# A spectral mixer with a GEGLU FFN on one core: LN1 reordered per quad, matmuls on zeros, W loaded in two halves, the last inverse n1 transform behind the first FFN chunk

## The chip, the cores and the metric

The kernel runs on one core of one Trainium2 chip. The time is device microseconds (us) of that core, lower is better.

The engines are TensorE (PE in the profile, with PEld for its weight loads), VectorE (DVE), ScalarE (ACT), GpSimd (POOL) and SyncE (SP). SyncE only issues transfers here; GpSimd issues the FFN's weight loads. The profile counts one set of 16 DMA engines for all transfers, whoever issues them. The granted clock is the share of full speed that TensorE's throttle lets through. LN1 and LN2 are the two layernorms, an eviction is a copy of matmul results out of PSUM, where TensorE leaves them, and a warm TensorE is one at full clock, a cold one at half.

## The reference, cut to what matters

```python
h  = x + irfft2(rfft2(layernorm(x)) * (w_r + 1j * w_i))          # x: 2048 x 576
h2 = h + (gelu(ln_h @ w_gate) * (ln_h @ w_up)) @ w_down           # ln_h = layernorm(h); 576 -> 4608 -> 576
```

The Fourier transforms are done as matmuls with tables. The kernel goes through these parts: LN1 and a transform along n1 (16 tiles in four quads), a transform along d and the product with W (16 groups), the inverse transforms (16 tiles), and the FFN in four blocks of 512 rows, each with 36 gate/up chunks of 18 matmuls and then the down matmuls.

## The kernel before

The first part works quad by quad: statistics on VectorE (three tiles) and ScalarE (one tile), a square root on ScalarE, a reciprocal, the scaling of the table ATS on GpSimd, 20 matmuls into PSUM, and five evictions into U.

```python
    ln1_act(0); ln1_stats(0); ln1_sqrt(0)
    ln1_act(1); ln1_stats(1); ln1_scale(0); ln1_sqrt(1)
    a_quad(0, (ACT, ACT, ACT, ACT, ACT))         # 20 matmuls, 5 evictions
    ln1_act(2); ln1_stats(2); ln1_scale(1); ln1_sqrt(2)
    a_quad(1, (ACT, ACT, DVE, ACT, DVE))
    # ... cut: quads 2 and 3 in the same way
```

SyncE issues x, the tables FT, BT and VT, then W in 18 loads, then the tables DT and IT. GpSimd waits for IT and DT and then issues the FFN's weights: gate and up (WGU), and the down weights (WD) once the place of U and W is free.

```python
    for pl, src in ((0, A_w_r), (1, A_w_i)):
        for jj in range(4):
            # ... cut: two loads per jj, 16 partitions x 16 (or 15) groups x 289 elements
            P.dma(SP, WS[jj:64:4, :, pl, 0:K2], a, f"w{pl}", r=["Wz"], w=[("W", pl, jj)])
    # ... cut
    P.op(POOL, None, r=["IT", "DT"])              # GpSimd waits
    for j in range(9):
        P.dma(POOL, WGU[0:64, :, f0:f1], wgv[:, :, f0:f1], f"wg{j}", w=[("WG", j, 0)])
        P.dma(POOL, WGU[64:128, :, f0:f1], wuv[:, :, f0:f1], f"wg{j}", w=[("WG", j, 1)])
    P.alias(ukeys + wkeys + [...], [("WD", j) for j in range(9)])
    for j in range(9):
        P.dma(POOL, WD[:, 4 * j:4 * j + 4, :], wdv[:, 4 * j:4 * j + 4, :], f"wd{j}", w=[("WD", j)])
```

During the inverse transforms the first four tiles are normalized and transposed on TensorE into HT0. Gate and up matmuls use 64 rows of TensorE each, so both partition halves need all of HT. A pair of transfers per tile copies what the other half has.

```python
    def turn_pe(c):
        # ... cut: five transposes on TensorE into PSUM, one eviction on VectorE
        P.dma(SP, HT0[0:64, 5:9, t0:t1], HT0[64:128, 0:4, t0:t1], f"tr{c}", r=[("HT", 0, c, 0)], w=[("HT", 0, c, 1)])
        P.dma(SP, HT0[64:128, 5:9, t0:t1], HT0[0:64, 1:5, t0:t1], f"tr{c}", r=[("HT", 0, c, 0)], w=[("HT", 0, c, 2)])

    for c in range(NT + 1):
        if c < NT:  st_I(c)                       # inverse along d
        if c >= 1:  st_N(c - 1)                   # inverse along n1, residual, sums for LN2
        # ... cut: LN2 of quads 0 to 2, norm() and turn_pe() of tiles 0 to 3
    ln2_a(3); ln2_b(3); ln2_c(3)
```

## Time and profile before

| | before |
|---|---|
| time, median of 4 runs | 532.30 us (531.28 to 533.65) |
| span of the profiled run | 530.8 us |
| first 128-wide matmul of the front | 12.42 us |
| first 289-wide matmul (transform along d) | 33.15 us |
| first 288-wide matmul (inverse along d) | 79.17 us |
| first gate/up matmul | 106.41 us |
| first down matmul | 176.5 us |

These are the rows of the profile page in 40 slices of 13.3 us: TensorE's busy tenths, its granted clock in tenths, the share of the DMA engines and what they moved.

```profile
PE   0379989999999999999999999999999999999997
PEclk9999999999999999999999999999999999999999
DMA  8979999401110000011100000111000000000000
GB/s 325 217 181 216 219 219 319 135 6 26 26 26 12 7 19 18 13 25 27 26 9 7 18 18 14 24 26 27 11 12 17 18 1 1 1 2 1 12 18 17
```

From slice 8 on (106 us) TensorE is full until the end, and the DMA engines are nearly idle; in the first seven slices the DMA engines are busy for 70% or more. All that can be won lies ahead of 106 us. The next lines are TensorE's timeline in the front (start, length, instruction, and in brackets how long the engine had been idle and for whom).

```profile
12.42 2.45 PE L426 MATMUL PS<-ATS,XO 128*128 128x128 bf16 x20 [12.42 <-POOL ATS L418]
...
33.15 4.99 PE L475 MATMUL PS<-FT,U 128*128 128x289 bf16 x20 [0.73 <-ACT U L438]
...
42.15 1.41 PE L475 MATMUL PS<-FT,U 128*128 128x289 bf16 x10
```

Twenty 289-wide matmuls take 4.99 us at first and ten take 1.41 us later, so the early ones run at little more than half the rate. The clock row shows 9 all along: the records of this run begin only at 38.9 us, so it says nothing of the time before.

The chain that ended last, from the fourth tile's eviction on (start, length, what):

```profile
102.65 0.74 DVE HT_69 L610
...
103.41 0.59 SPq L193
...
104.04 2.13 DMA HT_69<-HT_69
...
106.41 70.11 PE PS L649 x648
```

The FFN starts when the last copy of HT has landed, 2.13 us after it was issued. The two issue lines of W are (x9 each; shortest, median and longest issue in ns; first and last start):

```profile
L193 SPq DMA_DIRECT2D WS<-in_A_w_r_dram x9: 608/699/2300, 4.9 to 12.7; - x9
L193 SPq DMA_DIRECT2D WS<-in_A_w_i_dram x9: 595/609/684, 13.7 to 19.0; - x9
```

The table IT was issued at 20.3 us and landed 8.6 us later, near 28.9 us, GpSimd issued its first weight load soon after, and the first packet of WGU moved at 31.5 us:

```profile
29.85 0.92 POOL L193 DMA_DIRECT2D WGU<-in_B_w_gate_dram  x1
```

The last packet of WD moved at 97.8 us. In a window amid that stream the DMA view shows (packets, MB and share by queue; below it a transfer with its us from issue to landing):

```profile
q0 software_dynamic: 286, 1.17, 102.5%
...
HT_69<-HT_69 SPq DMA_DIRECT2D x2, 64.0 KB, 5.5
```

Queue q0 is GpSimd's, q1 SyncE's. The copies issued at 92.42 us and 93.14 us moved nothing in this window; they landed after 5.5 us (median of the two).

### The profile page before, as it was taken

How to read it: one execution, taken by the hardware profiler on the slowest of the kernel's cores; microseconds unless marked ns; L12 is line 12 of the kernel's file. 1: busy time of each engine (PE TensorE's matmuls, PEld its weight loads, DVE VectorE, ACT ScalarE, POOL GpSimd, SP SyncE). 2: the span in 40 equal slices, each digit the busy share in tenths (PEclk: the TensorE clock that was granted, in tenths of full speed). 3: DMA queues.
4: the chain of work that ended last, by engine and by line, in shares of the span. 5: the costliest groups of instructions: out<-in, count | busy, mean ns of one | idle time of the engine just before them, and what ended most of it. 6: DMA issues, size and time to landing. Idle time of an engine off the chain costs nothing.

```text
span 530.8 us, 10113 instructions
## 1 busy us (share of the span) xinstructions
PE 500.6 (94%) x4388; PEld 301.1 (57%) x4388; DVE 185.9 (35%) x427; ACT 151.1 (28%) x280; POOL 26.8 (5%) x40
## 2 busy tenths in 40 slices
PE   0379989999999999999999999999999999999997
PEld 0356757655555777444447774444477744444776
DVE  5337775844333211343332113433311133333111
ACT  4535557843323100233330003223300033332000
POOL 2182013000000000000000000000000000000000
PEclk9999999999999999999999999999999999999999
DMA  8979999401110000011100000111000000000000
GB/s 325 217 181 216 219 219 319 135 6 26 26 26 12 7 19 18 13 25 27 26 9 7 18 18 14 24 26 27 11 12 17 18 1 1 1 2 1 12 18 17
DMA packets 34395, 30.75 MB, mean 58 GB/s; under 512 B 21008, under 2 KB 29328, under 8 KB 34352
## 3 DMA queue, kind: packets, MB, share of 16 engines
q0 software_dynamic: 4176, 15.93, 12.5%
q1 hardware_dynamic: 30032, 13.66, 10.2%
q8 instruction: 34, 0.56, 0.4%
q10 hardware_dynamic: 144, 0.52, 0.3%
q14 instruction: 9, 0.07, 0.0%
HBM read 23.67 MB, written 2.36 MB: 49 GB/s over the span
## 4 chain that ended last, share of the span: by engine, by line
PE 91%; DVE 4%; DMA 1%; ACT 1%; POOL 1%; issue 0%; SPq 0%; DVEq 0%; POOLq 0%
PE PS L649 53%; PE PS L662 27%; PE PS L475 4%; PE PS L552 3%; PE PS L426 1%; PE PS L489 1%; DVE ST_53 L399 1%; PE PS L508 1%; DMA XO<-in_A_x_dram 1%; POOL ATS L418 1%; ACT U L438 1%; PE PS L512 1%; DVE XO L564 1%; PE PS L561 0%; DMA HT_69<-HT_69 0%
## 5 line engine op out<-in xcount | busy, mean ns | idle before, releaser
L653 ACT ACTIVATE GL<-PS 128x512 bf16<-128x512 f32 x144 | 86.0, 597 | 298.1 <-PE PS L649 295.4
L654 DVE TENSOR_TENSOR AT<-GL,PS 128x512 bf16<-128x512 bf16 x144 | 98.8, 688 | 169.5 <-ACT GL L653 169.5
L662 PE MATMUL PS<-WD,AT 128*128 128x288 bf16 x1152 | 141.8, 286 | 0.0
L649 PE MATMUL PS<-HT_69,WGU 64*128 64x512 bf16 x1296 | 140.2, 376 | 0.4 <-DMA HT_69<-HT_69 0.4
L649 PE MATMUL PS<-HT_83,WGU 64*128 64x512 bf16 x1296 | 140.2, 376 | 0.0
L662 PEld LDWEIGHTS PS<-WD,AT 128*128 128x128 bf16 x1152 | 112.4, 98 | 29.9 <-issue 1.7
L649 PEld LDWEIGHTS PS<-HT_69,WGU 64*128 64x128 bf16 x1296 | 68.3, 94 | 71.9 <-issue 0.9
L649 PEld LDWEIGHTS PS<-HT_83,WGU 64*128 64x128 bf16 x1296 | 62.9, 94 | 76.8 <-issue 0.5
L665 DVE TENSOR_TENSOR OS<-PS,XO 128x288 bf16<-128x288 f32 x32 | 14.7, 458 | 123.5 <-PE PS L662 123.5
L426 PE MATMUL PS<-ATS,XO 128*128 128x128 bf16 (+1 forms) x80 | 9.8, 312 | 22.6 <-POOL ATS L418 22.6
L475 PE MATMUL PS<-FT,U 128*128 128x289 bf16 x160 | 24.7, 307 | 0.7 <-ACT U L438 0.7
L552 PE MATMUL PS<-DT,V 128*128 128x288 bf16 x160 | 22.0, 286 | 0.5 <-ACT V L515 0.5
L426 PEld LDWEIGHTS PS<-ATS,XO 128*128 128x128 bf16 (+1 forms) x80 | 8.1, 148 | 24.1 <-POOL ATS L418 23.3
L475 PEld LDWEIGHTS PS<-FT,U 128*128 128x128 bf16 x160 | 15.4, 103 | 6.9 <-issue 0.9
L552 PEld LDWEIGHTS PS<-DT,V 128*128 128x128 bf16 x160 | 15.4, 98 | 4.3 <-issue 0.6
L564 DVE SCALAR_TENSOR_TENSOR XO<-PS,XO 128x576 bf16<-128x576 f32 x16 | 12.1, 757 | 8.6 <-PE PS L561 8.4
L590 DVE TENSOR_SCALAR HN<-XO,TM,RS_59 128x576 bf16<-128x576 bf16 (+1 forms) x32 | 10.2, 360 | 7.3 <-DMA HT_83<-HN 5.3
L567 ACT ACTIVATE SQ<-XO 128x576 bf16<-128x576 bf16 x16 | 10.9, 683 | 3.9 <-DVE XO L564 3.8
L508 PE MATMUL PS<-VT,ZS 128*128 128x256 bf16 x64 | 9.6, 271 | 2.0 <-DVE ZS L499 1.2
L481 ACT ACTIVATE CUS<-PS 128x289 bf16<-128x289 f32 x16 | 6.6, 414 | 16.7 <-PE PS L475 16.7
L494 DVE TENSOR_TENSOR T_78<-YS,WS 128x580 bf16<-128x580 bf16 x16 | 7.4, 461 | 11.0 <-ACT YS L492 11.0
L489 PE MATMUL PS<-CUS,BT 128*128 128x289 bf16 x64 | 11.1, 296 | 0.1
(52 smaller groups left out, 166.6 us busy)
## 6 DMA issues: line engine op xcount, KB each, us to landing
WGU<-in_B_w_gate_dram POOLq DMA_DIRECT2D x9, 576.0 KB, 22.3
WGU<-in_B_w_up_dram POOLq DMA_DIRECT2D x9, 576.0 KB, 24.3
WD<-in_B_w_down_dram POOLq DMA_DIRECT2D x9, 576.0 KB, 11.1
out_dram<-OS SPq DMA_DIRECT2D x32, 72.0 KB, 1.6
XO<-in_A_x_dram SPq DMA_DIRECT2D x3, 576.0 KB, 7.0
HT_83<-HN SPq DMA_TRANSPOSE x72, 2.4
FT<-c_ftab SPq DMA_DIRECT2D x1, 725.0 KB, 8.9
DT<-c_dtab SPq DMA_DIRECT2D x1, 720.0 KB, 8.0
```

Of the source, the lines that this page charges most:

```text
L426: P.op(PE, lambda t, b=b, w=w, i=i, c=c, dt=dt: t.matmul(bank(b, 0, w, 128 * i, 128 * i + 128), XO[:, c, 128 * dt:128 * dt + w], ATS[:, c, ...
L475: P.op(PE, lambda t, b=b, o=o, dt=dt, g=g: t.matmul(bank(b, 0, 128, 0, K2), U[:, dt, g, :, :], FT[:, dt, o, 0:K2], start=(dt == 0), stop=( ...
L489: P.op(PE, lambda t, b=b, o=o, tb=tabs[o], sl=sl, sp_=sp_: t.matmul(bank(b, 0, 128, 0, K2), BT[:, sp_, tb, :], CUS[:, sl, o, 0:K2], start= ...
L508: P.op(PE, lambda t, c=c, zp=zp, sl=sl, sp_=sp_: t.matmul(bank(6, 0, 128, 256 * c, 256 * c + 256), ZS[:, sl, zp, 128 * c:128 * c + 128], V ...
L552: P.op(PE, lambda t, b=b, h=h, kt=kt, c=c: t.matmul(bank(b, 0, 128, 0, 288), V[:, kt, c, :, :], DT[:, kt, 288 * h:288 * h + 288], start=(k ...
L564: P.op(DVE, lambda v, x2=x2, c=c: v.scalar_tensor_tensor(x2, banks(4, 2, 288), 1.0, x2, op0=ALU.mult, op1=ALU.add, accum_out=SB2[:, 0, c:c ...
L567: P.op(ACT, lambda a, sl=sl, c=c: a.activation(SQ[:, sl, :], XO[:, c, :], ACTF.Square, accum_out=SB2[:, 1, c:c + 1]), r=[("X", c)], w=[("S ...
L649: P.op(PE, lambda t, o=o, h0=h0, kt=kt, sl=sl, f=f, b0=b0, HT=HT: t.matmul(bank(b0 + o), WGU[h0:h0 + 64, kt, 128 * f:128 * f + 128], HT[h0 ...
L653: P.op(ACT, lambda a, s2=s2, b0=b0: a.activation(GL[:, s2, :], bank(b0), ACTF.Gelu_apprx_tanh), r=[("PS", b0)], w=[("GL", s2)])
L654: P.op(DVE, lambda v, s2=s2, b0=b0, f=f: v.tensor_tensor(AT[:, f, :], GL[:, s2, :], bank(b0 + 1), op=ALU.mult), r=[("GL", s2), ("PS", b0 + ...
L662: P.op(PE, lambda t, b0=b0, h=h, f=f, p=p: t.matmul(bank(b0 + h, 0, 128, 0, 288), AT[:, f, 128 * p:128 * p + 128], WD[:, f, 288 * h:288 * ...
L665: P.op(DVE, lambda v, b0=b0, h=h, p=p, c=c: v.tensor_tensor(OS[:, p % 2, 288 * h:288 * h + 288], bank(b0 + h, 0, 128, 0, 288), XO[:, c, 28 ...
```

## The change

It aims at the first 106 us. The statistics are interleaved so that only one VectorE tile of the next quad's stands before a quad's scale, not all three, the last quad's scale moves from GpSimd to VectorE, and ScalarE's table load for the square root goes to the start. Matmuls on a tile of zeros are to keep TensorE's clock up. W is loaded in two halves of its groups, so that the first product needs half of it. The last inverse n1 transform (st_N of tile 15) and LN2 of the last quad move behind the first FFN chunks, so that TensorE need not wait for them.

```diff
+    P.op(POOL, lambda g: g.memset(ZD[:, :], 0.0), w=["ZD"])
-    for pl, src in ((0, A_w_r), (1, A_w_i)):
-        # ... cut: 9 loads for each plane
+    for hf, (g0, g1) in enumerate(((1, 9), (9, 16))):
+        for pl, src in ((0, A_w_r), (1, A_w_i)):
+            # ... cut: 8 loads for each plane in the first half, 10 in the second
+    def idle_mm(n):
+        for _ in range(n):
+            P.op(PE, lambda t: t.matmul(bank(7), ZD[:, 0:128], ZD[:, :], start=True, stop=True), r=["ZD"], w=[("PS", 7)])
-    ln1_act(0)
-    ln1_stats(0)
-    # ... cut
+    P.op(ACT, lambda a: a.activation(SA[:, 0, 0:1], EPT[:, 0:1], ACTF.Sqrt), r=["EPT"], w=[("SA0", 0)])
+    ln1_act(0)
+    ln1_act(1)
+    idle_mm(24)
+    # ... cut: tile by tile, idle_mm(4) after quads 0, 1 and 2, idle_mm(3) after quad 3
-        if c >= 1:
+        if 1 <= c < NT:
             st_N(c - 1)
-    ln2_a(3)
-    ln2_b(3)
-    ln2_c(3)
+        if n == 0:                      # in gu(), after the matmuls of chunk 0
+            st_N(NT - 1)
+            P.alias(fdead, fnew)
+            if tb == 0 and f == 20:     # in the loop over chunks
+                ln2_a(3)
+                ln2_b(3)
+                ln2_c(3)
```

The copies of HT, the order of the weights' loads and the FFN's matmuls are not touched.

More of the change, by code (lines that the diff above doesn't have):

```diff
@@ L329, in _build @@
     JNK = sb.alloc("JNK", [128, 2, D], BF16)
+    ZD = sb.alloc("ZD", [128, 512], BF16)
     sb.off = v_off
@@ L365, in _build @@
     P.dma(SP, VT[:, :, :, :].rearrange("p a b c -> p (a b c)"), dram["VTAB"][:, :], "vt", w=["VT"])
-    for pl, src in ((0, A_w_r), (1, A_w_i)):
-        for jj in range(4):
-            a = bass.AP(src.tensor, 16 * jj * K2, [[128 * K2, 16], [K2, NG], [1, K2]])
-            P.dma(SP, WS[jj:64:4, :, pl, 0:K2], a, f"w{pl}", r=["Wz"], w=[("W", pl, jj)])
-            a = bass.AP(src.tensor, (64 + 16 * jj + 15) * K2, [[128 * K2, 16], [-K2, NG - 1], [1, K2]])
-            P.dma(SP, WS[64 + jj:128:4, 1:NG, pl, 0:K2], a, f"w{pl}", r=["Wz"], w=[("W", pl, 4 + jj)])
-        a = bass.AP(src.tensor, 64 * K2, [[128 * K2, 16], [16 * K2, 4], [1, K2]])
-        P.dma(SP, WS[64:128, 0, pl, 0:K2], a, f"w{pl}", r=["Wz"], w=[("W", pl, 8)])
+    for hf, (g0, g1) in enumerate(((1, 9), (9, 16))):
+        for pl, src in ((0, A_w_r), (1, A_w_i)):
+            for jj in range(4):
+                a = bass.AP(src.tensor, (16 * jj + g0) * K2, [[128 * K2, 16], [K2, g1 - g0], [1, K2]])
+                P.dma(SP, WS[jj:64:4, g0:g1, pl, 0:K2], a, f"w{pl}{hf}", r=["Wz"], w=[("W", hf, pl, jj)])
+                a = bass.AP(src.tensor, (64 + 16 * jj + 16 - g0) * K2, [[128 * K2, 16], [-K2, g1 - g0], [1, K2]])
+                P.dma(SP, WS[64 + jj:128:4, g0:g1, pl, 0:K2], a, f"w{pl}{hf}", r=["Wz"], w=[("W", hf, pl, 4 + jj)])
+            if hf:
+                for p0 in range(2):
+                    a = bass.AP(src.tensor, 64 * p0 * K2, [[128 * K2, 16], [16 * K2, 4], [1, K2]])
+                    P.dma(SP, WS[64 * p0:64 * p0 + 64, 0, pl, 0:K2], a, f"w{pl}{hf}", r=["Wz"], w=[("W", hf, pl, 8 + p0)])
     GORD = list(range(1, NG)) + [0]
-    wkeys = [("W", pl, h) for pl in range(2) for h in range(9)]
+    wkeys = [[("W", hf, pl, h) for pl in range(2) for h in range(8 + 2 * hf)] for hf in range(2)]
     P.dma(SP, DT[:, :, :].rearrange("p a b -> p (a b)"), dram["DTAB"][:, :], "dt", w=["DT"])
@@ L382, in _build @@
     P.op(POOL, lambda g: g.memset(ZS[:, :, :, K2:ZW], 0.0), w=["Zz"])
-    ACT_TILES = (1, 5, 9, 13)
     def ln1_act(q):
-        for c in range(4 * q, 4 * q + 4):
-            if c in ACT_TILES:
-                P.op(ACT, lambda a, c=c: a.activation(JNK[:, 0, :], XO[:, c, :], ACTF.Identity, accum_out=SA[:, 0, c:c + 1]),
-                     r=[("X", c)], w=[("SA0", c), "J0"])
-                P.op(ACT, lambda a, c=c: a.activation(JNK[:, 1, :], XO[:, c, :], ACTF.Square, accum_out=SA[:, 1, c:c + 1]),
-                     r=[("X", c)], w=[("SA1", c), "J1"])
@@ L395, in ln1_stats @@
-    def ln1_stats(q):
-        for c in range(4 * q, 4 * q + 4):
-            if c not in ACT_TILES:
-                for h in range(2):
-                    P.op(DVE, lambda v, c=c, h=h: v.bn_stats(ST1[:, c, h, :], XO[:, c, 288 * h:288 * h + 288]), r=[("X", c)], w=[("ST1", c, h)])
-        for c in range(4 * q, 4 * q + 4):
-            if c not in ACT_TILES:
-                P.op(DVE, lambda v, c=c: v.bn_aggr(MV1[:, c, :], ST1[:, c, :, :]), r=[("ST1", c, 0), ("ST1", c, 1)], w=[("MV1", c)])
-        for c in range(4 * q, 4 * q + 4):
-            if c in ACT_TILES:
-                P.op(DVE, lambda v, c=c: v.scalar_tensor_tensor(TM[:, 0, c:c + 1], SA[:, 0, c:c + 1], 1.0 / (D * D), SA[:, 0, c:c + 1],
-                                                                op0=ALU.mult, op1=ALU.mult), r=[("SA0", c)], w=[("TM", c)])
-                P.op(DVE, lambda v, c=c: v.scalar_tensor_tensor(MV1[:, c, 1:2], SA[:, 1, c:c + 1], 1.0 / D, TM[:, 0, c:c + 1],
-                                                                op0=ALU.mult, op1=ALU.subtract), r=[("SA1", c), ("TM", c)], w=[("MV1", c)])
+        c = 4 * q + 3
@@ new lines, in ln1_act, with ln1_tile @@
+        P.op(ACT, lambda a, c=c: a.activation(JNK[:, 0, :], XO[:, c, :], ACTF.Identity, accum_out=SA[:, 0, c:c + 1]),
+             r=[("X", c)], w=[("SA0", c), "J0"])
+        P.op(ACT, lambda a, c=c: a.activation(JNK[:, 1, :], XO[:, c, :], ACTF.Square, accum_out=SA[:, 1, c:c + 1]),
+             r=[("X", c)], w=[("SA1", c), "J1"])
+    def ln1_tile(c):
+        for h in range(2):
+            P.op(DVE, lambda v, c=c, h=h: v.bn_stats(ST1[:, c, h, :], XO[:, c, 288 * h:288 * h + 288]), r=[("X", c)], w=[("ST1", c, h)])
@@ new lines, in ln1_var @@
+    def ln1_var(q):
+        for c in range(4 * q, 4 * q + 3):
+            P.op(DVE, lambda v, c=c: v.bn_aggr(MV1[:, c, :], ST1[:, c, :, :]), r=[("ST1", c, 0), ("ST1", c, 1)], w=[("MV1", c)])
+        c = 4 * q + 3
+        P.op(DVE, lambda v, c=c: v.scalar_tensor_tensor(TM[:, 0, c:c + 1], SA[:, 0, c:c + 1], 1.0 / (D * D), SA[:, 0, c:c + 1],
+                                                        op0=ALU.mult, op1=ALU.mult), r=[("SA0", c)], w=[("TM", c)])
+        P.op(DVE, lambda v, c=c: v.scalar_tensor_tensor(MV1[:, c, 1:2], SA[:, 1, c:c + 1], 1.0 / D, TM[:, 0, c:c + 1],
+                                                        op0=ALU.mult, op1=ALU.subtract), r=[("SA1", c), ("TM", c)], w=[("MV1", c)])
@@ L413, in ln1_sqrt, with ln1_scale @@
              r=[("MV1", c) for c in range(4 * q, 4 * q + 4)] + ["EPT"], w=[("SD1", q)])
-    def ln1_scale(q):
+    def ln1_scale(q, eng):
         cs = slice(4 * q, 4 * q + 4)
         P.op(DVE, lambda v, cs=cs: v.reciprocal(RS1[:, cs], RS1[:, cs]), r=[("SD1", q)], w=[("RS1", q)])
-        P.op(POOL, lambda g, cs=cs: g.tensor_tensor(ATS[:, cs, :], ATB[:, cs, :], RS1[:, cs].unsqueeze(2).to_broadcast([128, 4, 128]), op=ALU.mult),
-             r=[("RS1", q), "ATB"], w=[("ATS", c) for c in range(4 * q, 4 * q + 4)])
+        if eng == POOL:
+            P.op(POOL, lambda g, cs=cs: g.tensor_tensor(ATS[:, cs, :], ATB[:, cs, :], RS1[:, cs].unsqueeze(2).to_broadcast([128, 4, 128]), op=ALU.mult),
+                 r=[("RS1", q), "ATB"], w=[("ATS", c) for c in range(4 * q, 4 * q + 4)])
+        else:
+            for c in range(4 * q, 4 * q + 4):
+                P.op(DVE, lambda v, c=c: v.tensor_scalar(ATS[:, c, :], ATB[:, c, :], RS1[:, c:c + 1], None, op0=ALU.mult),
+                     r=[("RS1", q), "ATB"], w=[("ATS", c)])
+    def idle_mm(n):
+        for _ in range(n):
+            P.op(PE, lambda t: t.matmul(bank(7), ZD[:, 0:128], ZD[:, :], start=True, stop=True), r=["ZD"], w=[("PS", 7)])
     def a_mm(q, dt):
-        b = (5 * q + dt) % 8
+        b = (5 * q + dt) % 7
         w = 128 if dt < 4 else 64
@@ L430, in a_ev @@
     def a_ev(q, dt, eng):
-        b = (5 * q + dt) % 8
+        b = (5 * q + dt) % 7
         w = 128 if dt < 4 else 64
@@ L438, in a_ev @@
             P.op(ACT, lambda a, s=src, d=dst: a.activation(d, s, ACTF.Copy), r=[("PS", b)], w=[("U", q, dt)])
-    def a_quad(q, engs):
-        for dt in range(5):
-            a_mm(q, dt)
-            a_ev(q, dt, engs[dt])
+    P.op(ACT, lambda a: a.activation(SA[:, 0, 0:1], EPT[:, 0:1], ACTF.Sqrt), r=["EPT"], w=[("SA0", 0)])
     ln1_act(0)
-    ln1_stats(0)
-    ln1_sqrt(0)
-    ln1_act(1)
-    ln1_stats(1)
-    ln1_scale(0)
-    ln1_sqrt(1)
-    a_quad(0, (ACT, ACT, ACT, ACT, ACT))
-    ln1_act(2)
-    ln1_stats(2)
-    ln1_scale(1)
+    ln1_act(1)
+    idle_mm(24)
+    for c in range(3):
+        ln1_tile(c)
+    ln1_var(0)
+    ln1_sqrt(0)
+    ln1_act(2)
+    ln1_tile(4)
+    ln1_scale(0, POOL)
+    ln1_tile(5)
+    ln1_tile(6)
+    ln1_var(1)
+    a_mm(0, 0)
+    a_ev(0, 0, ACT)
+    ln1_sqrt(1)
+    for dt in range(1, 5):
+        a_mm(0, dt)
+    a_ev(0, 1, ACT)
+    a_ev(0, 2, ACT)
+    ln1_tile(8)
+    ln1_scale(1, POOL)
+    ln1_tile(9)
+    ln1_tile(10)
+    ln1_var(2)
+    a_ev(0, 3, ACT)
+    a_ev(0, 4, ACT)
     ln1_sqrt(2)
-    a_quad(1, (ACT, ACT, DVE, ACT, DVE))
     ln1_act(3)
-    ln1_stats(3)
-    ln1_scale(2)
-    ln1_sqrt(3)
-    a_quad(2, (ACT, DVE, ACT, DVE, DVE))
-    ln1_scale(3)
-    a_quad(3, (ACT, DVE, ACT, DVE, ACT))
+    idle_mm(4)
+    for dt in range(5):
+        a_mm(1, dt)
+        a_ev(1, dt, ACT)
+    ln1_tile(12)
+    ln1_scale(2, POOL)
+    ln1_tile(13)
+    ln1_tile(14)
+    ln1_var(3)
+    ln1_sqrt(3)
+    idle_mm(4)
+    for dt in range(5):
+        a_mm(2, dt)
+    a_ev(2, 0, ACT)
+    a_ev(2, 1, DVE)
+    ln1_scale(3, DVE)
+    a_ev(2, 2, ACT)
+    a_ev(2, 3, DVE)
+    a_ev(2, 4, ACT)
+    idle_mm(4)
+    for dt in range(5):
+        a_mm(3, dt)
+        a_ev(3, dt, (ACT, DVE)[dt % 2])
+    idle_mm(3)
     ukeys = [("U", q, dt) for q in range(4) for dt in range(5)] + ["Uz"]
@@ L492, in st_B @@
         P.op(ACT, lambda a, sl=sl: a.activation(YS[:, sl, :, 0:K2], banks(4, 2, K2), ACTF.Copy), r=[("PS", 4), ("PS", 5)], w=[("Y", sl)])
-        wk = wkeys + ["Wz", "Yz", "Zz"]
+        wk = wkeys[0 if 1 <= g < 9 else 1] + ["Wz", "Yz", "Zz"]
         P.op(DVE, lambda v, g=g, sl=sl: v.tensor_tensor(T1[:, sl, :, :], YS[:, sl, :, :], WS[:, g, :, :], op=ALU.mult), r=[("Y", sl)] + wk, w=[("T1", sl)])
@@ L518, in st_V @@
              r=[("PS", 7), "Vfree"], w=[("Vt", g)])
-    P.alias(["ATB", "J0", "J1"] + [("ATS", c) for c in range(NT)], ["Vfree"])
+    P.alias(["ATB", "J0", "J1", "ZD"] + [("ATS", c) for c in range(NT)], ["Vfree"])
     for i in range(NG + 2):
@@ L538, in _build @@
         P.dma(POOL, WGU[64:128, :, f0:f1], wuv[:, :, f0:f1], f"wg{j}", w=[("WG", j, 1)])
-    P.alias(ukeys + wkeys + ["Wz", ("CU", 0), ("CU", 1), ("SU", 0), ("SU", 1)], [("WD", j) for j in range(9)])
+    P.alias(ukeys + wkeys[0] + wkeys[1] + ["Wz", ("CU", 0), ("CU", 1), ("SU", 0), ("SU", 1)], [("WD", j) for j in range(9)])
     for j in range(9):
@@ L629, in _build @@
             turn_pe((c - 7) // 2)
-    ln2_a(3)
-    ln2_b(3)
-    ln2_c(3)
     fdead = vkeys + ["DT", "IT", ("G", 0), ("G", 1), ("Y", 0), ("Y", 1), "Yz", "Zz", ("SQ", 0), ("SQ", 1)]
     fdead += [("T1", a) for a in range(2)] + [(n_, a, b_) for n_ in ("T2", "Z") for a in range(2) for b_ in range(2)]
-    P.alias(fdead, [("AT", f) for f in range(36)] + [("GL", 0), ("GL", 1)] + [("HT", 1, i, k) for i in range(4) for k in range(9)])
+    fnew = ([("AT", f) for f in range(36)] + [("GL", 0), ("GL", 1)] + [("HT", 1, i, k) for i in range(4) for k in range(9)])
     GT = (0, 5, 1, 6, 2, 7, 3, 8, 4)
```

## The prediction

> **What bounds it now.** The timeline of before falls into a front (0 to 33.15 us, LN1 and first transform), a spectral part (33.15 to 106.4) and an FFN (106.4 to 530.8) in which TensorE never waits (groups view: 70.1 us per gate/up block, 35.4 per down block, idle 0.4). The change doesn't touch the FFN's matmuls, so only the start of the first gate/up matmul, 106.41, can move.
>
> **Front.** The chain of waits alternates statistics (377 ns each), square root (0.30), GpSimd scale (1.03), 20 matmuls (2.46) and evictions (0.50 to 0.69). The table load at 7.04 (1.28 us) goes to the start, ScalarE takes tile 3 of each quad. Replaying the new order with these durations: first scaled table at about 10.8 instead of 12.4, last eviction about 22 instead of 33; ScalarE's evictions limit.
>
> **Warm clock.** In before the 128-wide matmuls are about 122 ns apart, and the first twenty 289-wide ones take 4.99 us, against 1.34 per ten later. (The clock row shows 1.00 throughout.) The Trainium skill ("TensorE: Matmul & The Clock Gate", Part 1) puts that down to a clock at half rate until about 3.4 us of activity; this trace agrees in the factor (250 to 134 ns). If zeros count as activity, the first transforms gain another 2.8 us. W in halves: first half lands at about 20 to 22 (before: W landings 14 to 26), first use about 26, so no stall.
>
> Together the spectral part starts 10.8 us earlier and is 2.8 shorter: 13.6 us at the last inverse transform.
>
> **Where the gain goes.** The first gate/up matmul waits for the copies of transposed tiles between partition halves (HT from HT, SyncE queue), not for the last n1 transform. Gate, up and down weights don't move earlier: DMA share is 1.0 from 6 to 96 us; the down weights land until 98, and should land at 97 to 99 again. In before, the copies issued at 92.4 amid that stream moved no byte until 95.8 and landed after 5.2 to 5.8 us; the last, in silence, took 2.1. Now all four pairs (issued about 79 to 90) meet the stream. The skill ("DMA: Bandwidth & Descriptors", Queues, rings and completion order) says rings take turns by packets; a copy then waits a turn of large descriptors (212 to 310 ns each in this trace). My estimate is some 4.4 us per pair, so the last lands at 96 to 101, about 98.5, instead of 93. TensorE idles some 7 us, cools, and the FFN starts at half rate: +2.
>
> **Tail order.** The last n1 transform behind the first chunk puts 0.25 us of matmuls there and delays the first GELU (eviction 0.76, square 0.87, table load 1.28, GELU 0.6, multiply 0.69 after the chunk): third chunk's banks come late by about 0.5. Square root in chunk 20: two table loads (2.6 us) hidden by three bank pairs of 1.95 us each.
>
> Sum: -7.9 + 2 + 0.75, about -5.5 us; without the DMA collision 519.7.
>
> **Predicted: 527.0 us, 80% range 520.3 to 530.7. Faster by over 2%: 0.17, within 2%: 0.81, slower: 0.02.**
>
> **Right or wrong:** the 289-wide matmuls start at 21 to 25 and the first twenty take about 2.7 us; the 288-wide inverse ones start near 65.5; HT copies take over 5 us; the first gate/up matmul idles several us on DMA HT; the first nine pairs of it take twice as long; no ScalarE stall in chunk 20.
>
> **What would make it wrong:** copies passing the weights quicker (towards 520), or starving until the weights end (towards 531); zeros that don't warm; W's descriptors delaying DT and IT, and with them the weights.

## The result, and the profile after

The changed kernel takes 535.90 us (median of 4 runs, 535.68 to 536.22), against 532.30 us. The ratio is 1.0067, with a 95% interval of 1.0043 to 1.0090. Ratios here are the mean time of one kernel's runs over that of the kernel before's runs of the same rounds, so not quite the ratio of the medians. The change made the kernel a little slower, and the time lies outside the predicted range.

| start of | before | after | difference |
|---|---|---|---|
| first 128-wide matmul | 12.42 | 10.74 | -1.7 |
| first 289-wide matmul | 33.15 | 21.37 | -11.8 |
| first 288-wide matmul | 79.17 | 64.99 | -14.2 |
| first gate/up matmul | 106.41 | 106.52 | +0.1 |
| first down matmul | 176.5 | 179.8 | +3.3 |

The front did what it was made for, and 14.2 us are won at the inverse transforms. At the first gate/up matmul nothing of it is left. The page's rows:

```profile
PE   7999897099999999999999999999999999999997
PEclk9999999589999999999999999999999999999999
DMA  8669999801110000011100000111000000000000
GB/s 326 137 169 215 215 216 270 273 1 26 26 26 17 7 18 18 9 26 28 24 14 6 18 18 12 26 26 26 11 7 18 18 6 1 1 1 2 12 18 18
```

Slice 7 (93.5 to 106.8 us) is empty for TensorE, the granted clock falls to half there, and the DMA engines are busy one slice longer than before. The front in the timeline:

```profile
1.32 7.19 PE L428 MATMUL PS<-ZD 128*128 128x512 bf16 x24 [1.32 <-POOL ZD L356]
...
10.74 1.52 PE L435 MATMUL PS<-ATS,XO 128*128 128x128 bf16 x20 [2.23 <-POOL ATS L419]
...
21.37 2.63 PE L513 MATMUL PS<-FT,U 128*128 128x289 bf16 x20
...
35.45 0.92 POOL L193 DMA_DIRECT2D WGU<-in_B_w_gate_dram  x1 [19.43 <-DMA IT<-c_itab]
```

The matmuls on zeros run from 1.32 us, twenty 128-wide ones take 1.52 us in place of 2.45, and twenty 289-wide ones 2.63 us in place of 4.99. They did not keep the clock up throughout: its records show half from 11.90 to 15.31 us, and the second quad's twenty 128-wide matmuls, at 13.88 us, took 2.09 us. The last line is the other side: GpSimd's first weight load waits for IT until 35.45 us, where before it was issued at 29.85 us. W's issue lines tell why:

```profile
L193 SPq DMA_DIRECT2D WS<-in_A_w_r_dram x18: 594/600/1249, 4.9 to 21.8; - x18
L193 SPq DMA_DIRECT2D WS<-in_A_w_i_dram x18: 593/599/777, 10.2 to 28.3; - x18
```

Eighteen more loads cost SyncE about 0.6 us each, though each moves half as much (the issue of a half load takes 600 ns, that of a whole one 609 ns at the median of its second plane). SyncE is through with W at 28.9 us instead of 19.6; IT is issued at 29.6, lands 5.2 us later, near 34.8, and the first packet of WGU moves at 37.1 us instead of 31.5. The last packet of WD moves at 104.8 us instead of 97.8.

The chain that ended last, around the start of the FFN:

```profile
88.47 0.73 DVE HT_69 L648
...
90.23 16.04 DMA HT_69<-HT_69
...
106.52 4.03 PE PS L683 x18
110.54 0.55 PE PS L599 x2
...
111.11 0.78 DVE XO L602 x2
...
112.71 1.28 ACT L690
...
114.63 0.70 DVE AT L691
...
115.38 64.41 PE PS L683 x593
```

The last copy of HT takes 16 us, from 90.23 us on, where before it took 2.13. The DMA view in ten microseconds of that wait:

```profile
q0 software_dynamic: 787, 3.20, 95.8%
q1 hardware_dynamic: 786, 0.19, 9.5%
...
HT_69<-HT_69 SPq DMA_DIRECT2D x1, 64.0 KB, 16.0
```

The two queues moved the same number of packets, 787 and 786: one copy packet of 256 B or less for each packet of the weights, most of which are 4608 B and take about 220 ns. The copies are 2048 packets of 256 B with 128 small ones for completion, so at 79 packets a microsecond they would need 27 us, longer than the weights last. In the trace their first packet moved at 84.8 us and their last at 105.7 us: by 103.0 us 1340 of the 2176 packets had moved, and the other 836 went in the last 2.7 us, as the weights ran out. The 16 us of the last copy are thus mostly the turns of the pairs ahead of it in SyncE's queue.

The windows view (us; busy us and number of instructions for PE, PEld, DVE, ACT, POOL; clock, DMA share, GB/s) of a stretch of the front, of the wait, and of the first chunks after it:

```profile
8.49:11.90 3.41, 1.18 (x20) 1.06 (x20) 3.18 (x14) 2.86 (x10) 1.03 (x1) 1.00 1.01 411
91.00:106.50 15.50, 0.00 (x0) 0.01 (x1) 0.26 (x2) 1.00 (x3) 0.00 (x0) 0.59 0.94 289
106.50:115.40 8.90, 8.78 (x59) 3.30 (x61) 1.53 (x4) 3.19 (x6) 0.00 (x0) 0.75 0.01 2
```

The mean granted clock is 0.59 in the wait and 0.75 in the first chunks. The chain says what that and the new tail cost. The 18 matmuls of chunk 0 take 4.03 us, against 1.95 in a warm chunk (70.11 us over 36): +2.1. The moved n1 transform puts 0.47 us between chunk 0 and chunk 1 (110.54 to 111.01). Then a chunk waits at 115.38 us for the multiply of chunk 0, which comes late behind residual, square, table load and GELU. The whole gate/up block takes 73.27 us (106.52 to 179.79) against 70.11, so +3.16; less 2.08 and 0.47 that leaves 0.6 us for this wait. With +0.11 at the start it makes the 3.3 us by which the span is longer.

### The profile page after: what moved, and what is told of

The parts are those of the page before. It is cut to its first block, busy times and chain, and to the rows that moved or that the text cites. A ratio compares the mean times of both kernels' runs of the same rounds, so it can differ in the third digit from the quotient of the medians.

```text
span 534.1 us, 10212 instructions
## 1 busy us (share of the span) xinstructions
PE 508.4 (95%) x4427; PEld 296.4 (55%) x4427; DVE 184.2 (34%) x428; ACT 152.8 (29%) x285; POOL 26.3 (5%) x40
## 4 chain that ended last, share of the span: by engine, by line
PE 91%; DMA 4%; DVE 3%; ACT 1%; issue 1%; POOL 0%; SPq 0%; DVEq 0%; POOLq 0%
PE PS L683 52%; PE PS L699 27%; PE PS L513 4%; DMA HT_69<-HT_69 3%; PE PS L590 3%; PE PS L527 1%; PE PS L546 1%; PE PS L435 1%; DMA XO<-in_A_x_dram 1%; PE PS L428 1%; DVE XO L602 1%; PE PS L550 1%; PE PS L599 1%; ACT JNK L392 0%; DVE HT_69 L648 0%
## 5 line engine op out<-in xcount | busy, mean ns | idle before, releaser
L683 PEld LDWEIGHTS PS<-HT_69,WGU 64*128 64x128 bf16 x1296 | 63.4, 95 | 94.7 <-issue 18.7
L683 PEld LDWEIGHTS PS<-HT_84,WGU 64*128 64x128 bf16 x1296 | 62.9, 94 | 76.8 <-issue 0.5
L513 PE MATMUL PS<-FT,U 128*128 128x289 bf16 x160 | 22.3, 287 | 0.0
L428 PE MATMUL PS<-ZD 128*128 128x512 bf16 x39 | 12.0, 462 | 1.3 <-POOL ZD L356 1.3
L399 DVE BATCH_NORM_STATS2 ST_53<-XO 128x6 f32<-128x288 bf16 x24 | 9.2, 443 | 5.6 <-DMA XO<-in_A_x_dram 5.6
L530 ACT ACTIVATE YS<-PS 128x578 bf16<-128x578 f32 x16 | 10.5, 656 | 1.5 <-PE PS L527 0.3
L592 ACT ACTIVATE GS<-PS 128x576 bf16<-128x576 f32 x16 | 10.2, 635 | 2.6 <-PE PS L590 2.6
```

The lines of the kernel that those rows point to most:

```text
L428: P.op(PE, lambda t: t.matmul(bank(7), ZD[:, 0:128], ZD[:, :], start=True, stop=True), r=["ZD"], w=[("PS", 7)])
L513: P.op(PE, lambda t, b=b, o=o, dt=dt, g=g: t.matmul(bank(b, 0, 128, 0, K2), U[:, dt, g, :, :], FT[:, dt, o, 0:K2], start=(dt == 0), stop=( ...
L530: P.op(ACT, lambda a, sl=sl: a.activation(YS[:, sl, :, 0:K2], banks(4, 2, K2), ACTF.Copy), r=[("PS", 4), ("PS", 5)], w=[("Y", sl)])
L683: P.op(PE, lambda t, o=o, h0=h0, kt=kt, sl=sl, f=f, b0=b0, HT=HT: t.matmul(bank(b0 + o), WGU[h0:h0 + 64, kt, 128 * f:128 * f + 128], HT[h0 ...
```

## The experiments

Theory A: the copies of HT take turns with the weight loads packet for packet and so end only when those end; the front's gain turns into a wait for them. Rivals: B, the 36 loads of W alone are to blame; C, the wait has nothing to do with W; D, the copies get nothing at all until the weights are through; E, the copies have a fixed rate. The moved tail is tested by itself. Kernels of one set ran on one chip, with runs of the kernel before beside them (medians 532.60, 532.92 and 532.63 us in the three sets).

### W loaded as before, in the changed kernel

```diff
-    for hf, (g0, g1) in enumerate(((1, 9), (9, 16))):
-        # ... 36 loads
+    for pl, src in ((0, A_w_r), (1, A_w_i)):
+        # ... 18 loads
```

> The changed kernel with W loaded as before (18 loads, not 36). Theory A (the half-to-half copies of HT take turns, packet for packet, with the weight loads, and end when these end): SyncE is through with W near 19.6 us instead of 28.9, IT lands near 29 instead of 34.8, the weight loads start 5.5 to 6.5 us earlier and end near 98.5, the first gate/up matmul starts at 99 to 101 instead of 106.5, whole time about 529 to 530.5. It stays well short of 520, since the copies still meet the stream. Rival B (the 36 loads alone are to blame; with them gone the copies pass quickly): first gate/up matmul near 93, time near 520. Rival C (the wait has nothing to do with W): 535.9.

Measured: 529.02 us (528.17 to 529.86), ratio 0.9935 (0.9912 to 0.9959). WGU's first packet moved at 31.4 us, WD's last at 97.7 us, the copies' packets from 85.1 to 99.0 us. The chain:

```profile
92.41 7.16 DMA HT<-HT
...
99.81 3.81 PE PS L680 x18
```

The FFN starts at 99.81 us, as theory A has it, and 6.7 us earlier than in the changed kernel. B and C fall: the loads of W are nearly half of the matter, but the last copy still takes 7 us where it took 2. (This profiled run, like those of the single pair of copies and of the old tail below, also had 3.4 us at half clock, here from 65.7 us on; the changed kernel's had no such stretch there. My estimate of its cost is 1.7 us at most, half of 3.41, and it lies ahead of a wait for the copies; no run isolates it.) The run also shows what the halves are good for. The first product with W waited for W as a whole:

```profile
26.76 0.46 DVE L529 TENSOR_TENSOR T<-YS,WS 128x580 bf16<-128x580 bf16 x1 [2.76 <-DMA WS<-in_A_w_i_dram]
```

In the changed kernel it started at 25.72 us, so the halves save 1.0 us there.

### The down weights after the copies, in the changed kernel

```diff
+    P.op(POOL, None, r=[("HT", 0, c, k) for c in range(4) for k in (1, 2)])
     for j in range(9):
         P.dma(POOL, WD[:, 4 * j:4 * j + 4, :], wdv[:, 4 * j:4 * j + 4, :], f"wd{j}", w=[("WD", j)])
     # these loads now stand after the loop over the inverse transforms
```

> The changed kernel, W still in 36 loads, but the down weights are issued only after the copies of HT have landed. Theory A: the copies meet only the tail of the gate/up loads (until about 88), the last lands near 92.5, the first gate/up matmul starts at 92.5 to 94 with a warm clock, time 519 to 521.5. Rival B (W's 36 loads are what costs, through late gate/up weights or late tables): no better than the changed kernel, 534 to 536.

Measured: 520.26 us (520.10 to 520.52), ratio 0.9772 (0.9748 to 0.9795). The timeline around the start of the FFN:

```profile
92.07 2.12 PE L685 MATMUL PS<-HT,WGU 64*128 64x512 bf16 x18 [1.77 <-DMA HT<-HT]
92.41 6.71 POOL L193 DMA_DIRECT2D WD<-in_B_w_down_dram  x9 [43.66 <-DMA HT<-HT]
```

TensorE waits 1.77 us instead of 16.06, chunk 0 takes 2.12 us, the clock is up, and the down weights land by about 110 us, over 50 us ahead of the first down matmul at 163.6 us. W was still in 36 loads and WGU as late as in the changed kernel (first packet at 37.1 us), so B falls for good. The moving of nine loads is worth 15.6 us.

### One pair of copies for four tiles, in the changed kernel

```diff
-        P.dma(SP, HT0[0:64, 5:9, t0:t1], HT0[64:128, 0:4, t0:t1], ...)    # for each tile c
-        P.dma(SP, HT0[64:128, 5:9, t0:t1], HT0[0:64, 1:5, t0:t1], ...)
+        if c == 3:
+            P.dma(SP, HT0[0:64, 5:9, :], HT0[64:128, 0:4, :], ...)
+            P.dma(SP, HT0[64:128, 5:9, :], HT0[0:64, 1:5, :], ...)
```

> The changed kernel, with one pair of copies for all four tiles (pieces of 1 KB, 512 of them) in place of four pairs (pieces of 256 B, 2048 of them), issued after the fourth tile, near 89.5. Theory A (one small packet for each weight packet, about 75 a microsecond): about 7 us of turns after 2 to 6 us of start, landing at 99 to 102.5, first gate/up matmul 4 to 7 us earlier than 106.5, time 529 to 532. Rival D (the copies starve until the weights are through): first gate/up matmul still at 104.5 to 106.5, time 534 to 536.

Measured: 529.89 us (528.28 to 531.00), ratio 0.9949 (0.9922 to 0.9977). The copies were issued at 90.4 and 91.0 us, and the FFN started at 100.19 us, though WD's last packet moved only at 105.6 us. D falls. My count of packets was wrong: the trace shows 128 packets of 4096 B, not 512 of 1 KB. The DMA view of their window:

```profile
q0 software_dynamic: 138, 0.57, 59.2%
q1 hardware_dynamic: 128, 0.45, 46.0%
```

Again about as many packets of one queue as of the other. What did not fall with the count is the wait for the first turn: their first packet moved at 94.7 us, 4.2 us after the issue, where a copy in silence in the kernel before took 1.25 us (103.41 to 104.66). The run also speaks against E: at the changed kernel's 79 packets a microsecond the 128 packets would have gone in 1.6 us, at its 0.19 MB in 10 us their 0.52 MB would have taken 28 us, and the copies' share of the DMA engines was 9.5% there, not 46%. They took 4.5 us (94.7 to 99.2).

### The tail as before, in the changed kernel

```diff
-        if 1 <= c < NT:
+        if c >= 1:
             st_N(c - 1)
+    ln2_a(3); ln2_b(3); ln2_c(3)           # ahead of the FFN again
-        if n == 0:
-            st_N(NT - 1)
```

> The changed kernel with the tail as before: last n1 transform ahead of the first chunk, LN2 of the last quad there too. The first gate/up matmul still waits for the copies until about 106.5. Theory: the two 288-wide matmuls and the late banks of the third chunk are gone from the FFN, which is worth 0.8 to 1.1 us: 534.8 to 535.1. If the moved transform did help as intended, it would be slower than 535.9.

Measured: 534.85 us (533.29 to 535.53), ratio 1.0041 (1.0015 to 1.0067), 1.05 us under the changed kernel's median. The timeline:

```profile
105.36 8.02 PE L688 MATMUL PS<-HT,WGU 64*128 64x512 bf16 x59 [12.15 <-DMA HT<-HT]
```

TensorE still waits for the copies. The difference of about 1 us fits the moved tail's two terms above (0.47 and 0.6) but doesn't show that it is theirs: the two kernels were not timed in the same set, and in this profiled run, the fastest of the four, WD's last packet moved at 103.4 us instead of 104.8 and the FFN started 1.2 us earlier. The pair further down is of one set.

### The tail as before, with late down weights

The edit is the one above, on the version with late down weights.

> The version with the late down weights (520.3), with the tail as before. There the first gate/up matmul waits 1.8 us for the copies with nothing to do; the last n1 transform fits into that wait. Theory: its 0.4 us of matmuls and the 0.8 us for which chunk 3 waits for its banks leave the FFN: 518.8 to 519.6. If the moved transform is worth something as intended: slower than 520.3.

Measured: 519.40 us (518.87 to 520.45), ratio 0.9756 (0.9723 to 0.9790). That this is the tail's doing had to be shown in one set, with more rounds:

> The version with the late down weights once more, as base of the next two: 520.1 to 520.6.

> Late down weights and the tail as before, once more and in more rounds: 0.7 to 1.2 us faster than the base of the same rounds, 519.0 to 519.6; the best version yet.

Measured in the same rounds: 520.10 us (519.48 to 521.04) with the moved tail, 518.68 us (518.67 to 518.99) with the tail as before, a difference of 1.4 us, a little over the expected 0.7 to 1.2. The last n1 transform fits into the time in which TensorE has nothing to do:

```profile
91.45 0.40 PE L596 MATMUL PS<-GS,IT 128*128 128x288 bf16 x2 [0.95 <-DVE XO L599]
92.28 6.00 PE L690 MATMUL PS<-HT,WGU 64*128 64x512 bf16 x54 [0.42 <-DMA HT<-HT]
```

It ends ahead of the first chunk at 92.28 us, and that chunk waits only 0.42 us. The version is the best of all: ratio 0.9745 (0.9727 to 0.9763).

### No matmuls on zeros, with late down weights

```diff
-    idle_mm(24)        # and the four others
```

> The version with the late down weights, without any matmul on zeros. Theory (zeros count as activity and keep the clock up): the 128-wide matmuls of the front go back to about 122 ns apart, the first twenty 289-wide ones to about 5 us; start of these 0.5 to 1.5 us later, 2.8 us more behind it, in all 523 to 525. Rival (the zeros only take TensorE's time; 4.5 us of them stand in the chain of waits of the changed kernel): 516 to 520.

Measured: 521.01 us (519.54 to 522.40), ratio 0.9780 (0.9746 to 0.9813). The expected 523 to 525 was missed. The profiled run is the slowest of the four:

```profile
10.60 2.45 PE L435 MATMUL PS<-ATS,XO 128*128 128x128 bf16 x20 [10.60 <-POOL ATS L419]
13.41 2.34 PE L435 MATMUL PS<-ATS,XO 128*128 128x128 bf16 x20 [0.36 <-POOL ATS L419]
16.11 1.60 PE L435 MATMUL PS<-ATS,XO 128*128 128x128 bf16 x20 [0.36 <-POOL ATS L419]
18.93 2.62 PE L435 MATMUL PS<-ATS,XO 128*128 128x128 bf16 x20 [1.23 <-DVE ATS L423]
22.28 4.30 PE L508 MATMUL PS<-FT,U 128*128 128x289 bf16 x20 [0.73 <-ACT U L447]
```

In it, the first, second and fourth quads are slow (2.34 to 2.62 us), the third is not (1.60), and the twenty 289-wide matmuls take 4.30 us. The FFN starts at 94.83 us instead of 92.07. So in this run the zeros were worth 2.8 us, about as predicted, but hardly in every run: the third quad shows that the front without them can come warm by itself, and the fastest run, 519.54 us, is no slower than those with zeros (520.10 to 520.52). (The fronts of the faster runs were not profiled.) A comparison with more rounds, on the version with the old tail:

> The best version without the matmuls on zeros. In the earlier look without them the first quads were cold, but the shorter front came warm by itself at times (times from 519.5 to 522.4). Expected: 0.5 to 2.5 us slower than the best version, 519.8 to 521.5, and a wider spread. If the zeros are useless: the same median.

Measured: 520.55 us (519.07 to 521.66), against 518.68 us with the zeros in the same rounds. The zeros are worth 1.9 us at the median, and the spread falls from 2.6 to 0.3 us. That they stand in the chain of the changed kernel cost nothing on balance: without them the first 289-wide matmul starts at 22.28 us, not earlier.

### W loaded as before, with late down weights

The edits of the first two experiments together.

> Late down weights and W loaded as before. The weights' loads start 5.6 us earlier, but nothing waits for them; W lands as a whole near 26.3, 1 us after the first multiply by it could start. So the two halves are worth about 1 us where the copies don't gate: 521 to 521.8, against 520.3. If the 36 loads cost time of their own: faster than 520.3.

Measured: 521.59 us (521.23 to 523.34), ratio 0.9797 (0.9767 to 0.9828), 1.3 us above the late down weights alone in the set before. That agrees with the two halves being worth about 1 us once the copies don't gate. The two were not in one set, and the profiled run of this one also had 3.4 us at half clock from 65.1 us on, so the exact size stays open; the first 288-wide matmul starts at 65.53 us, 0.7 us later than with the halves (64.83).

### Control: late down weights in the kernel before

> Control: the kernel before, with the down weights issued only after the copies. Its last copies ran in silence anyway (2.1 us), so nothing moves: 532 to 533. If late down weights help by themselves (for instance by leaving the memory to the others): below 530.

Measured: 532.97 us (531.18 to 533.44), ratio 0.9998 (0.9967 to 1.0030). Late down weights are worth nothing where the last copies run in silence anyway. They pay only together with the faster front.

### Smaller loads of the down weights, in the changed kernel

```diff
     for j in range(9):
-        P.dma(POOL, WD[:, 4 * j:4 * j + 4, :], ...)
+        for i in range(2):
+            P.dma(POOL, WD[:, 4 * j + 2 * i:4 * j + 2 * i + 2, :], ...)
```

> The changed kernel, its down weights in 18 loads of two chunks (packets of 2304 B) in place of 9 of four (4608 B), the same bytes, issued at the same place. Theory A (one copy packet for each weight packet): a turn of the stream gets shorter, so the copies move 110 to 150 packets a microsecond amid the down weights instead of 75, and the last lands at 100 to 103.5 instead of 106; time 531 to 534. Rival E (the copies have a fixed share or rate, whatever the weights' packets): 75 a microsecond and 535.9 as before.

Measured: 535.50 us (534.72 to 536.28), ratio 1.0059 (1.0039 to 1.0080). As a test of the packets' size it failed: the trace shows that the weights still moved in packets of 4608 B. What doubled are the small completion packets of these loads. The time is nearer to what E expected than to A's 531 to 534, but with the packets unchanged the time can't tell the two apart. The DMA view in the same ten microseconds as of the changed kernel:

```profile
q0 software_dynamic: 860, 3.17, 95.2%
q1 hardware_dynamic: 860, 0.21, 10.5%
```

The copies moved 860 packets where they moved 786, exactly as many as the other queue, which had more packets in all. This speaks for turns and against a fixed rate (E), but only over a range of 9%. How the turns go with much smaller weight packets stays open.

## Why the prediction was wrong

Its ground plan was right: the front gets faster, the copies of HT meet the weights, TensorE cools in the wait, and the new tail costs a little. It was wrong in the size of one term, the landing of the last copy: 106.3 us instead of 98.5, which is 7.8 of the 8.9 us between 527.0 and 535.90.

- **Front: right.** Predicted for the 289-wide matmuls 21 to 25 us and 2.7 us for the first twenty; measured 21.37 and 2.63. For the inverse transforms 65.5; measured 64.99. (The stage between became 2.4 us shorter, not 2.8, and starts 11.8 us earlier, not 10.8.)
- **The step that failed: "the down weights land until 98, and should land at 97 to 99 again", and from it "the last lands at 96 to 101, about 98.5".** WD's last packet moved at 104.8 us and the last copy's at 105.7. Two sizes were off.
  - The weights came 5.6 us later at their start and 7.0 us later at their end, since SyncE pays about 0.6 us per load of W, half or whole, and IT stands behind 36 loads. The prediction named this among what could make it wrong, and did not cost it, although the issue times were in the trace of before (0.6 us for W's loads, 0.43 us for IT, in pieces of 4096 B where W's are 578 B).
  - The estimate "some 4.4 us per pair" came from turns of several descriptors, as the Trainium skill's page "DMA: Bandwidth & Descriptors" (Queues, rings and completion order) has them. Here the turns were single packets of the trace, 787 against 786. A pair is 544 packets, so at 79 a microsecond it takes 6.9 us. Four pairs would be 27 us, so they weren't through when the weights ran out, and it is the weights' end that set the landing.
- With W in 18 loads, and all else as changed, the time was 529.02 us, inside the predicted range of 520.3 to 530.7. So the late weights are what carried the time past the range. In that run the last copy landed at 99.6 us, inside the predicted 96 to 101, and that is luck as far as the second size goes: until 95 us the copies moved 761 packets in 9.9 us, as slowly as in the changed kernel, and the rest in 4 us as the weights ran out.
- **"without the DMA collision 519.7": about 0.1% off, in part by luck.** With the down weights late it was 520.26. Two misses nearly cancel there: the FFN started 14.3 us earlier, not 13.6, and in the profiled run its first gate/up block took 1.5 us longer, not 0.75.
- **Cooling: right.** Predicted +2 after some 7 us idle; chunk 0 took 4.03 us against 1.95, after 16 us idle. The skill's page "TensorE: Matmul & The Clock Gate" (Part 1) has the clock fall to half after an idle window of about 3.4 us; this trace agrees: it is at half for 17 us from 93.82 us on, after a window of that length (90.41 to 93.82) in which TensorE was busy for 0.05 us.
- **Tail: right in kind, a little small.** Predicted 0.75; the two terms measured 0.47 and 0.6, and the pair in one set 1.4 us. LN2 in chunk 20 showed no wait, as predicted: by the windows view TensorE was busy for 64.40 of the 64.40 us from 115.4 to 179.8 us.
- **Zeros: too large.** Predicted 2.8 us; worth 1.9 us at the median where the start of the FFN hardly waits for the copies. In the changed kernel, where the copies gate, they should be worth nothing; no run without them tested that.

## What to carry to other kernels

When a faster stage moves small transfers on the critical path into the time of a bulk load, count packets and not bytes: here the small ones got one turn for each large one, and 14 us were lost in a wait that no line of the change touches. Hold back a bulk load whose use is far off (the down weights had over 50 us to spare) until the small transfers have landed; with this and the old tail the same change gives 518.68 us instead of 535.90. Splitting a load makes what stands behind it in the issue queue later, so put what others wait for ahead of it or check its landing.

## What the Trainium skill lacked or had wrong

- "DMA: Bandwidth & Descriptors" (Queues, rings and completion order) says that an engine drains a whole packet of about 9 to 17 descriptors from one ring before it takes the next. Counted in the packets of this trace, SyncE's and GpSimd's queues went one for one: 787 against 786 and 860 against 860 in 10 us, with packets of 256 B against 4608 B. Whether the page means another kind of packet can't be told from here; a planner who reckons with turns of several of the trace's packets, as the prediction did, makes a small copy amid a bulk load too short (4.4 us for a pair that took 6.9).
- I found on that page no figure for the first turn of a queue beside a busy one. In these runs a copy's first packet moved 3.4, 4.2 and 6.6 us after its issue amid weight loads, and 1.25 us after it in silence. What makes the difference is not settled.
- I found there no cost of issuing many small loads from SyncE: in these runs about 0.6 us for each load of W, the same for half the bytes (600 and 609 ns at the median).
- "TensorE: Matmul & The Clock Gate" (Part 1) says that the clock falls after at least one idle window. In the changed kernel it fell to half at 11.9 us after a window of 3.41 us (8.49 to 11.90) in which TensorE was busy for 1.18 us by the windows view. So, if the windows run in step with the clock's records, a window need not be empty. Nor does the busy time alone decide: with W as before and late down weights the clock fell after a window with 1.93 us (61.70 to 65.11), and with late down weights alone it stayed up after one with 1.64 us (90.20 to 93.61).
- The page doesn't say whether zeros count as activity for the clock (it speaks of them for the current limit only). They do here: the matmuls on zeros start 0.42 us apart and are 0.21 us apart from the tenth on, 3.8 us after the first; the first record of the clock, at 5.07 us, says full speed.
